# Paired eviction of narrow MLP column tiles, scaled V copies on GpSimd and a new planner table in an attention and token-MLP kernel

## The chip, the cores and the metric

The kernel runs on one core of one Trainium2 chip. Its time is device time in microseconds (us). The kernel before takes 757.67 us, the median of three runs (757.1 to 758.49).

## What is computed

The input x has 2048 tokens of 640 features, all in bf16. With xn = layernorm(x), the kernel computes x + s * g, where s is multi-head attention over xn (32 heads of 20 features) and g = silu of a token-mixing MLP of xn. The MLP multiplies along the tokens: 2048 to 1536, gelu, back to 2048. Cut to what matters:

```python
xn = _layernorm(x, axis=-1)
# attention A: H = 32, Dh = 20
q, k, v = split(xn @ wqkv)
p = softmax(einsum("bhqd,bhkd->bhqk", q, k) * Dh ** -0.5)
s = merge_heads(einsum("bhqk,bhkd->bhqd", p, v)) @ wo
# token MLP B, on xn normalised once more
h = _layernorm(xn, axis=-1)
u = gelu(einsum("bsd,sf->bdf", h, w1) + b1)
g = silu(transpose(einsum("bdf,fs->bds", u, w2) + b2))
return x + s * g
```

## The kernel before

**Attention.** Heads are taken in 8 groups of four, and a group in passes of 512 queries: 32 passes. A pass has 16 key chunks of 128 for each of four heads, 64 units; a unit is one score tile of 128 keys by 512 queries in one bank of PSUM. TensorE makes the scores (L1212, heads at four row positions of the array) and multiplies the exponentials with V into one accumulator bank (L1292, four heads at four column positions).

**Two ways to an exponential.** ACT takes two or three units per instruction (`emit_exp`, L1230, L1241). DVE takes quads: four heads of one key chunk, which must be one of the five in `RC`. It adds an offset to each score and writes it as a 16-bit integer whose bits, read as bf16, are roughly a power of two (`emit_op1`, L1252, four for a quad). Three more versions, shifted by 32, 64 and 96 steps of that integer, are made in one instruction of 2048 columns each (`emit_top`, L1276, three for a quad). The PV matmul then takes four versions in turn, with V and with three scaled copies of V, so that their sum averages out the error of the coarse exponential. The scaled copies are `vs_sb`, made in `vs_steps` (L751): three instructions for a head group, each over five key chunks of 88 columns, 440 together. Group 0 is done chunk by chunk at the start, 15 instructions of 88 columns; groups 1 to 7 are done three instructions each. `vs_sb` holds two groups, so those of group G wait until the PV matmuls of group G-2 are done.

**MLP.** `mlp_steps` (L791) computes 128 output rows j over 640 feature columns. The 640 are split into a part of 512 (part 0, one bank for each j) and a part of 128 (part 1). Two neighbouring j share a bank for part 1, side by side, and the instruction on L815 then evicts each of them: times one half, plus a bias that depends on j and the partition. The target is `zt_sb`, one half for even and one for odd j. `act_steps` (L822) applies gelu or silu to the pair. The weights come in pieces of 256 columns, 512 bytes a row (`dma_w1`, L771; `dma_w2`, L778), into two alternating buffers in `regA`.

**What sets the order of the work.** Nothing is decided on the chip. `schedule` runs a planner when the kernel is built: it keeps a clock for each engine, gives every step a cost in ns (`dv`, `dp`, `ac`, `mm` at L452 to L462, and the number at the end of each step), and always takes the earliest ready candidate of the earliest engine, by priority. A DMA's cost is its bytes at 355 bytes a ns (L476). The result is one fixed instruction list for each engine; `Prog._add` derives the semaphore waits. Jobs have a due time in passes (`at`), which spreads projections and MLP over the attention. All jobs compete with the scores for banks and engines: five banks are in two groups for ACT (three and two), one belongs to DVE, one is the accumulator, one serves jobs.

**The table.** `PLAN` (L317) has 129 rows of 14 digits. Every 16 units `tune` (L412) sets 14 options of the planner from the next row (`OPTS`, L301): how much slack a job may take ahead of ACT's deadline, whether DVE may take quads, from what DVE load on an ACT bank is lent to it, the sizes in which quads are accumulated, and more.

Of the kernel before, what the change touches and what calls it, by code (L numbers as in the profile page):

```python
# [7 lines left out]
ALU = mybir.AluOpType  # L8
AF = mybir.ActivationFunctionType

P = 128
# [249 lines left out]
class _Kern:  # L261
# [53 lines left out]
        ("GROT", (1, 0)),  # L315
    )
    PLAN = (  # L317
        "00000000000010", "00000000000000", "00000000000010", "00000000000000", "00000410000000", "10010410000100",
        "00004010011000", "20204010111000", "00000000000000", "02000020010010", "00000000000000", "00000010001000",
        "00000000000000", "01000120000000", "01003120000000", "00000000000000", "00000010000100", "00000310100000",  # L320
        "02020320011000", "02020320011000", "02120010011000", "00000220000100", "30000220000100", "02000010000000",
        "00000000000000", "00000000100000", "02000100100100", "01000120001010", "00000000000000", "00003300000000",
        "00000000000000", "01000000000010", "00004000000000", "10011000000000", "01022300000000", "00000000000000",
        "30020100000000", "02000010110000", "00000100000000", "00010100000110", "00001000000000", "20100000000100",
        "11000000000000", "00000000000000", "00001000010000", "10020000000000", "10020000010000", "10020010010000",
        "00000000000000", "22103000000000", "22103010000000", "01220100000100", "00000000000000", "00100000001000",
        "02000000100000", "01000300001000", "01000300001000", "00000000000000", "00100000001000", "00100400100000",
        "01000000001000", "00004000000000", "10002000010000", "01001400001010", "01021420000110", "00000300000000",
        "00000020000010", "00000000000000", "00000010001000", "10000100000000", "10000100000000", "10004100001000",
        "00004120000000", "00001010000000", "10011410000110", "11001200000110", "11001200100110", "00020000000000",  # L330
        "00000000000000", "00000000100100", "00200400100000", "02100010110010", "02101010100010", "01000000000000",
        "01000000000000", "00000000000000", "00000400000000", "00000000000000", "00000020001000", "00020320000000",
        "00000000000000", "01000010000000", "01000010000100", "20000000000100", "02000000000000", "12000000000000",
        "00001000101000", "00000000000000", "00200000010100", "00020020100000", "01003000000000", "22000000000000",
        "21210000000000", "00000000000000", "00200020110000", "00000000000000", "00200000000100", "00000000001000",
        "00020310000100", "00220020000010", "10224000000010", "31223410000010", "30200000000100", "00021000000010",
        "00100000001010", "01100000010010", "01204001000000", "01204100001000", "00204100000010", "02024120000000",
        "02024320000000", "02000200000000", "12000200010000", "00000000000000", "00001000100000", "00001000100000",
        "00000000001000", "10000000000000", "00000000000000",
    )  # L340
    PARTS = (2,)
    DX = (1, 2, 3)
# [74 lines left out]
    def schedule(self):  # L417
        pr, t, nc = self.prog, self.t, self.nc
        S, NB, NTB, F, FC, D, H, DH, NG, GH = (self.S, self.NB, self.NTB, self.F, self.FC, self.D,
                                               self.H, self.DH, self.NG, self.GH)  # L420
# [4 lines left out]
        wp_sb, zt_sb = t["wp_sb"], t["zt_sb"]  # L425
# [13 lines left out]
        def S_(name):  # L439
            s = sl.get(name)  # L440
            if s is None:
                s = sl[name] = _Slot(name)
            return s

        bank_slot = [S_(f"bank{i}") for i in range(8)]

        def ps(b, n=512, off=0):
            return ps_all[:, b * 512 + off:b * 512 + off + n]
# [3 lines left out]
        def mm(n):  # L452
            return max(n / 2.4 + 3.0, 60.0)

        def dv(n, rate=1.04):
            return 65.0 + n * rate

        def dp(n):
            return 66.0 + n * 1.04
# [291 lines left out]
        def vs_steps(G, rs):  # L751
            half = 0 if G < 2 else 1
            steps = []
            r0, n = rs[0], len(rs)
            for k in range(3):
                src = bass.AP(v_sb, (RC[r0] * H + G * 4) * 22, [[NB * H * 22, P], [(RC[1] - RC[0]) * H * 22, n], [1, 88]])
                dst = vs_sb[:, G % 2, k, r0:r0 + n, :]
                steps.append(("dve", lambda e, src=src, dst=dst, k=k: e.tensor_scalar(dst, src, self.AK[k + 1], None, ALU.mult),
                              [S_(f"v{half}_{RC[r]}") for r in rs], [S_(f"vs{G % 2}_{k}_{r}") for r in rs],
                              f"vs{G}", dv(88 * n, 0.51)))  # L760
            for r in rs:
                steps.append(("tag", f"vs{G}_{r}"))
            return steps

        def w1_ap(k):
            return bass.AP(regA, (k % 2) * NB * 256, [[NB * 640, P], [256, NB], [1, 256]])
# [4 lines left out]
        def dma_w1(k):  # L771
            src = B_w1[:, k * 256:(k + 1) * 256].rearrange("(b p) f -> p b f", p=P)
            dst = w1_ap(k)
            wr = [S_(f"wm{k % 2}")]
            return ("dma", lambda e: e.dma_start(dst, src), [], wr, f"dma_w1_{k}", S * 512,
                    [S_(f"x{b}") for b in range(NB)] if k < 2 else [])

        def dma_w2(k):  # L778
            src = B_w2[:, k * 256:(k + 1) * 256].rearrange("(fc p) s -> p fc s", p=P)
            dst = w2_ap(k)  # L780
            wr = [S_(f"wn{k % 2}")]
            return ("dma", lambda e: e.dma_start(dst, src), [], wr, f"dma_w2_{k}", F * 512,
                    [S_("wm0"), S_("wm1")] if k < 2 else [])

        def ztmp(i):
            return zt_sb[:, i % 2, 0, :]
# [4 lines left out]
        def mlp_steps(which, j, part):  # L791
            def make(bk):
                steps = []
                if which == 1:
                    wap, rows, nk = w1_ap(j // 2), regC, NB
                    rd = [S_(f"wm{(j // 2) % 2}")] + [S_(f"h{b}") for b in range(NB)]
                    bias, sb_ = b1h_sb, S_("b1h")
                else:
                    wap, rows, nk = w2_ap(j // 2), regB, FC
                    rd = [S_(f"wn{(j // 2) % 2}")] + [S_(f"gelu{f}") for f in range(FC)]  # L800
                    bias, sb_ = b2h_sb, S_("b2h")
                c0, n = (0, 512) if part == 0 else (512, 128)
                js = (j,) if part == 0 else (j - 1, j)
                for i, jj in enumerate(js):
                    col0 = (jj % 2) * 128
                    for k in range(nk):
                        steps.append(pcol(lambda a, b_, i=i: ps_all[a:b_, bk * 512 + i * n:bk * 512 + i * n + n],
                                          wap[:, k, col0:col0 + 128], rows[:, k, c0:c0 + n], k == 0, k == nk - 1, rd,
                                          [bank_slot[bk]], f"m{which}_{j}", mm(n)))
                for i, jj in enumerate(js):  # L810
                    if jj >= 2:
                        steps.append(("need", f"a{which}_{jj - 2}"))
                    z = ztmp(jj)
                    zw = [S_(f"z{jj % 2}_{part}")]
                    steps.append(("dve", lambda e, z=z, i=i, jj=jj: e.tensor_scalar(  # L815
                        z[:, c0:c0 + n], ps(bk, n, i * n), 0.5, bias[:, jj:jj + 1], ALU.mult, ALU.add),
                        [bank_slot[bk], sb_], zw, f"m{which}e_{j}", dp(n) + 60.0))
                    steps.append(("tag", f"m{which}_{jj}_{part}"))
                return steps
            return make  # L820
# [617 lines left out]
        for i, (b0, nb) in enumerate(LN):  # L1438
            rq = () if i < 4 else (f"xn{LN[i - 1][0] + LN[i - 1][1] - 1}",)
            steps = ln_steps(b0, nb)  # L1440
            k = next(n for n, x in enumerate(steps) if x == ("tag", f"lnp{b0}")) + 1
# [16 lines left out]
        for w in (1, 0):  # L1458
            src = A_wqkv[:, 640 * w + 256:640 * w + 640].rearrange("(kc p) f -> p kc f", p=P)
# [63 lines left out]
        for j in range(FC):  # L1523
# [6 lines left out]
            if j % 2 == 1 and j // 2 + 2 < FC // 2:  # L1530
                k = j // 2 + 2
# [4 lines left out]
        for j in range(NB):  # L1536
# [6 lines left out]
            if j % 2 == 1 and j // 2 + 2 < NB // 2:  # L1543
                k = j // 2 + 2
# [12 lines left out]
        for gb in range(4):  # L1557
            src = A_x[0, gb * 512:(gb + 1) * 512, :].rearrange("(b p) d -> p b d", p=P)
            dst = regA[:, gb * 4:(gb + 1) * 4, :]
# [377 lines left out]
        while True:  # L1937
# [40 lines left out]
            r, e = bt  # L1978
# [46 lines left out]
```

The softmax here doesn't subtract the row's maximum and nothing guards it: scores larger than these inputs give would overflow.

## Time and profile before

The profiled execution took 758.22 us; its span from the first to the last instruction is 756.4 us, at a granted TensorE clock of 1.0.

| engine | busy us | share | instructions |
|---|---|---|---|
| ScalarE (ACT) | 731.3 | 97% | 686 |
| TensorE (PE) | 726.6 | 96% | 10194 |
| VectorE (DVE) | 718.4 | 95% | 1319 |
| GpSimd (POOL) | 15.7 | 2% | 22 |

In a row of the profile's table of groups, a line number, an engine and an operation are followed by what is written and read, the shape, the count, then busy time in us, the mean of one in ns, and the engine's idle time just before these instructions with what ended most of it. In the views of waits, a row has the waiting engine and line, what it waited for, and the total in us, the number of times and the longest wait.

### The profile page before, as it was taken

The numbers are of one execution on the slowest core, as the hardware profiler recorded it, in microseconds if no ns is written. First come the engines' busy times: TensorE is split into PE (matmuls) and PEld (weight loads), VectorE is DVE, ScalarE is ACT, GpSimd is POOL, SyncE is SP. The second block draws the span as 40 slices with busy tenths as digits, with TensorE's granted clock in tenths as the row PEclk, the third lists the DMA queues.
The fourth block names the chain that finished last, engine by engine and source line by source line (L and its number), as shares of the span: only waits on it lengthen the run. The fifth ranks groups of instructions, "written<-read, shape, count | busy, mean of one in ns | idle before, by whom it ended". The sixth has DMA issues, their size and how long they took to land.

```text
span 756.4 us, 22917 instructions
## 1 busy us (share of the span) xinstructions
PE 726.6 (96%) x10194; PEld 245.9 (33%) x10194; DVE 718.4 (95%) x1319; ACT 731.3 (97%) x686; POOL 15.7 (2%) x22
## 2 busy tenths in 40 slices
PE   8899999999999999999999989999999899999997
PEld 6332233222332323323232233333333333322232
DVE  7799999999999999999999999999999898999996
ACT  4999999999999999999999999999999999999994
POOL 4200000000000000000000000000000000000001
PEclk9999999999999999999999999999999999999999
DMA  8694111101120302203010131331134510410002
GB/s 240 89 160 88 41 20 37 21 13 30 37 63 12 76 13 44 62 26 76 13 39 13 37 91 31 69 80 29 45 81 76 104 50 2 152 47 29 31 13 70
DMA packets 117143, 42.54 MB, mean 56 GB/s; under 512 B 75300, under 2 KB 115876, under 8 KB 116996
## 3 DMA queue, kind: packets, MB, share of 16 engines
q1 hardware_dynamic: 117044, 41.07, 24.2%
q8 instruction: 80, 1.31, 0.8%
q14 instruction: 19, 0.16, 0.1%
HBM read 26.37 MB, written 10.22 MB: 48 GB/s over the span
## 4 chain that ended last, share of the span: by engine, by line
ACT 67%; PE 23%; SPq 4%; DVE 3%; DMA 3%; POOL 1%; issue 0%; DVEq 0%; ACTq 0%
ACT pt_sb L1241 65%; PE ps_all L1212 7%; PE ps_all L1292 7%; PE ps_all L645 7%; SPq L906 3%; DMA xnT_sb<-regC 1%; PE ps_all L930 1%; DMA regA<-in_B_w_dram 1%; ACT zt_sb L836 1%; DMA wqk_sb<-in_A_wqkv_dram 1%; DVE dt_sb L1252 1%; PE ps_all L630 1%; POOL st_sb L567 0%; SPq L1425 0%; DVE regC L1615 0%
## 5 line engine op out<-in xcount | busy, mean ns | idle before, releaser
L1241 ACT ACTIVATE pt_sb<-ps_all 128x1024 bf16<-128x1024 f32 (+1 forms) x662 | 711.5, 1212 | 3.9 <-PE ps_all L1212 2.9
L1252 DVE TENSOR_SCALAR dt_sb<-ps_all 128x512 uint16<-128x512 f32 x496 | 330.8, 681 | 17.1 <-PE ps_all L1212 15.6
L1212 PE MATMUL ps_all<-qk_sb 32*128 32x512 bf16 x2048 | 286.6, 384 | 18.7 <-ACT pt_sb L1241 14.5
L1276 DVE TENSOR_SCALAR dt_sb<-dt_sb 128x2048 uint16<-128x2048 uint16 x372 | 245.9, 684 | 1.6
L1212 PEld LDWEIGHTS ps_all<-qk_sb 32*128 32x128 bf16 x2048 | 73.9, 91 | 276.4 <-ACT pt_sb L1241 193.0
L1292 PE MATMUL ps_all<-pt_sb,v_sb 128*21 128x512 bf16 x1552 | 123.6, 382 | 1.0 <-DVE v_sb L1045 1.0
L1292 PE MATMUL ps_all<-dt_sb,vs_sb 128*21 128x512 bf16 x1488 | 123.6, 381 | 0.3 <-DVE dt_sb L1276 0.2
L645 PE MATMUL ps_all<-regB,regA 128*32 128x128 bf16 (+1 forms) x1536 | 66.8, 301 | 1.5 <-DMA regA<-in_B_w_dram 1.2
L645 PE MATMUL ps_all<-regC,regA 128*32 128x512 bf16 (+1 forms) x1536 | 65.9, 301 | 0.0
L1292 PE MATMUL ps_all<-dt_sb,v_sb 128*21 128x512 bf16 x496 | 48.9, 385 | 0.6 <-DVE tr_sb L1408 0.3
L645 PE MATMUL ps_all<-xnT_sb,wqk_sb 128*32 128x512 bf16 x640 | 48.9, 382 | 0.3 <-DVE v_sb L1045 0.2
L1292 PEld LDWEIGHTS ps_all<-pt_sb,v_sb 128*21 128x21 bf16 x1552 | 29.1, 90 | 50.6 <-issue 38.5
L1292 PEld LDWEIGHTS ps_all<-dt_sb,vs_sb 128*21 128x21 bf16 x1488 | 31.6, 91 | 38.2 <-issue 18.8
L645 PEld LDWEIGHTS ps_all<-regB,regA 128*32 128x32 bf16 x1536 | 28.1, 96 | 28.5 <-issue 12.2
L645 PEld LDWEIGHTS ps_all<-regC,regA 128*32 128x32 bf16 x1536 | 28.5, 96 | 25.7 <-issue 11.7
L930 PE MATMUL ps_all<-wv_sb,xnT_sb 128*128 128x128 bf16 (+3 forms) x160 | 30.1, 302 | 0.1
L645 PE MATMUL ps_all<-wv_sb,xnT_sb 128*32 128x480 bf16 x320 | 23.6, 369 | 0.2 <-DVE v_sb L1045 0.2
L1408 DVE STREAM_TRANSPOSE tr_sb<-ps_all 128x512 f32<-128x512 f32 x31 | 21.9, 707 | 0.0
L645 PEld LDWEIGHTS ps_all<-xnT_sb,wqk_sb 128*32 128x32 bf16 x640 | 14.3, 95 | 20.0 <-issue 8.7
L1292 PEld LDWEIGHTS ps_all<-dt_sb,v_sb 128*21 128x21 bf16 x496 | 12.4, 90 | 23.7 <-issue 18.3
L815 DVE TENSOR_SCALAR zt_sb<-ps_all,b2h_sb 128x512 bf16<-128x512 f32 (+1 forms) x32 | 17.2, 543 | 1.4 <-PE ps_all L645 1.2
L1045 DVE CAST v_sb<-ps_all 128x480 bf16<-128x480 f32 (+1 forms) x24 | 14.3, 594 | 2.3 <-PE ps_all L738 2.1
(81 smaller groups left out, 291.0 us busy)
## 6 DMA issues: line engine op xcount, KB each, us to landing
regA<-in_B_w_dram SPq DMA_DIRECT2D x6, 1024.0 KB
regA<-in_B_w_dram SPq DMA_DIRECT2D x8, 768.0 KB
qk_sb<-qk_scratch_dram SPq DMA_DIRECT2D x56, 80.0 KB
qk_scratch_dram<-qs_sb SPq DMA_DIRECT2D x32, 128.0 KB
regA<-in_A_x_dram SPq DMA_DIRECT2D x6, 640.0 KB
ok_scratch_dram<-on_sb SPq DMA_DIRECT2D x96, 20.0 KB
out_dram<-regC SPq DMA_DIRECT2D x3, 640.0 KB
wqk_sb<-in_A_wqkv_dram SPq DMA_DIRECT2D x2, 480.0 KB
```

The lines of the kernel that those rows point to most:

```text
L630: steps.append(("pe", lambda e, dc=dc, lhsT=lhsT: e.matmul(ps(bk, n), lhsT, xnT_sb[:, dc, tb * 512 + c0:tb * 512 + c0 + n], start=(dc == 0 ...
L645: fns.append(lambda e, c=c, e_=e_: e.matmul(oc(c, e_), lhsT[:, c:e_], rhs, start=start, stop=stop, tile_position=(0, c)))
L815: steps.append(("dve", lambda e, z=z, i=i, jj=jj: e.tensor_scalar(z[:, c0:c0 + n], ps(bk, n, i * n), 0.5, bias[:, jj:jj + 1], ALU.mult, AL ...
L906: steps.append(("dma", lambda e, d=d, src=src: e.dma_start_transpose(d, src), [S_(f"okd{pass_of[(G, tb)]}_{g}") for G in range(L6) for g i ...
L930: steps.append(("pe", lambda e, c=c, k=k: e.matmul(ap, oT_sb[0:k, c, b * 128:(b + 1) * 128], wo_ap[0:k, c, c0:c0 + n], start=(opens and c ...
L1045: return lambda e: e.tensor_copy(dst, src)
L1212: pr.pe(lambda e, outp=outp, lhsT=lhsT, rhs=rhs, g=g: e.matmul(outp, lhsT, rhs, start=True, stop=True, tile_position=(32 * g, 0)), reads=[ ...
L1241: tk = pr.act(lambda e: e.activation(outp, inp, AF.Exp, scale=math.log(2.0) / 128.0), reads=[bank_slot[b] for b in banks[:n]], writes=[S_( ...
L1252: tk = pr.dve(lambda e: e.tensor_scalar(w, src, WOFF, 0.0, ALU.add, ALU.max), reads=[bank_slot[bk]], writes=[S_(f"dt{d['tl'][0]}_{g}")], n ...
L1276: tk = pr.dve(lambda e: e.tensor_scalar(dst, src, dk, None, ALU.add), reads=[S_(f"dt{b0}_{g}") for g in range(4)], writes=[S_(f"dt{b}_{g}" ...
L1292: pr.pe(lambda e: e.matmul(outp, lhsT, rhs, start=(k == 0), stop=last, tile_position=(0, 32 * g)), reads=reads, writes=[bank_slot[AB]], na ...
L1408: steps.append(("dve", lambda e: e.transpose(tr_sb[:, :], ps(AB)), [bank_slot[AB]], [S_("tr")], f"epT{q}", 632.0))
```

## The change

It has four parts.

1. `mlp_steps`: the two 128-column parts of a pair are evicted by one instruction of 2 x 128 columns. The bias is no longer a scalar for each partition but a second tensor operand, read with a step of zero along the columns.
2. `vs_steps`: the scaled V copies of groups 1 to 7 go to GpSimd, with a planned cost of 700 ns. Group 0 stays on DVE.
3. `dma_w1` and `dma_w2`: the planner counts 922 instead of 512 bytes for each row of weights. The transfers themselves are as before.
4. `PLAN`: a new table, of which four of the 129 rows equal the old ones at their place.

The first two are for taking work off DVE, the third for a truer picture of the weight loads in the planner, and the table fits the planner's choices to the new costs.

```diff
     PLAN = (
-        "00000000000010", "00000000000000", "00000000000010", "00000000000000", "00000410000000", "10010410000100",
...
+        "00010000000000", "02000000000000", "00000000000000", "00000020100100", "20104000000000", "10000000011000",
...
     )
@@ vs_steps
-                steps.append(("dve", lambda e, src=src, dst=dst, k=k: e.tensor_scalar(dst, src, self.AK[k + 1], None, ALU.mult),
+                steps.append(("pool" if G else "dve", lambda e, src=src, dst=dst, k=k: e.tensor_scalar(dst, src, self.AK[k + 1], None, ALU.mult),
                               [S_(f"v{half}_{RC[r]}") for r in rs], [S_(f"vs{G % 2}_{k}_{r}") for r in rs],
-                              f"vs{G}", dv(88 * n, 0.51)))
+                              f"vs{G}", 700.0 if G else dv(88 * n, 0.51)))
@@ dma_w1
-            return ("dma", lambda e: e.dma_start(dst, src), [], wr, f"dma_w1_{k}", S * 512,
+            return ("dma", lambda e: e.dma_start(dst, src), [], wr, f"dma_w1_{k}", S * 922,
@@ dma_w2
-            return ("dma", lambda e: e.dma_start(dst, src), [], wr, f"dma_w2_{k}", F * 512,
+            return ("dma", lambda e: e.dma_start(dst, src), [], wr, f"dma_w2_{k}", F * 922,
@@ mlp_steps
-                for i, jj in enumerate(js):
+                for jj in js:
                     if jj >= 2:
                         steps.append(("need", f"a{which}_{jj - 2}"))
+                if part:
+                    zp = zt_sb[:, :, 0, c0:c0 + n]
+                    bp = bass.AP(bias, j - 1, [[FC if which == 1 else NB, P], [1, 2], [0, n]])
+                    pp = ps(bk, 2 * n).rearrange("p (i n) -> p i n", i=2)
+                    steps.append(("dve", lambda e: e.scalar_tensor_tensor(zp, pp, 0.5, bp, ALU.mult, ALU.add),
+                                  [bank_slot[bk], sb_], [S_("z0_1"), S_("z1_1")], f"m{which}e_{j}", dp(2 * n) + 60.0))
+                    for jj in js:
+                        steps.append(("tag", f"m{which}_{jj}_{part}"))
+                    return steps
+                for i, jj in enumerate(js):
```

More of the change, by code (lines that the diff above doesn't have):

```diff
@@ L317 @@
     PLAN = (
-        "00000000000010", "00000000000000", "00000000000010", "00000000000000", "00000410000000", "10010410000100",
[L319 to L337, printed above, removed]
@@ L338 @@
-        "02024320000000", "02000200000000", "12000200010000", "00000000000000", "00001000100000", "00001000100000",
-        "00000000001000", "10000000000000", "00000000000000",
+        "00010000000000", "02000000000000", "00000000000000", "00000020100100", "20104000000000", "10000000011000",
+        "11003000110000", "00101000000000", "00000000000000", "02003100000000", "00000200000000", "00100200000000",
+        "00104200000000", "20104200100000", "00000000000000", "20102000100000", "20102000100100", "00000000000000",
@@ new lines @@
+        "00000000100000", "00021010100000", "30020020100000", "30020020110000", "10220020100000", "02100200000000",
+        "02000000000010", "11000000010000", "11000000110000", "11000100110100", "11002100110100", "00000020010000",
+        "00000000000000", "01020400101010", "00000220010000", "00000400000000", "00000300001000", "02120320001000",
+        "01103000001000", "01202020001000", "00000000000000", "00020000001000", "01014300010100", "01214420010100",
+        "00000000000000", "00200300001000", "00020010000000", "00000000000000", "02000000010000", "02000100001010",
@@ new lines @@
+        "00023010100010", "00223010100010", "00100010101000", "00203010001000", "00102000001000", "00000200110010",
+        "10000300110110", "00000000000000", "01100300000000", "00020000000010", "00000000000000", "10100000000000",
+        "20020000000000", "20020200001000", "00020400101000", "00100400000000", "00120420000100", "11100300100100",
+        "00020010001000", "00100000100000", "00000010000000", "21004200000000", "00000100000000", "00000000000000",
+        "02200000000000", "02200010010000", "10200010110010", "12200010110000", "00100000001000", "00000220000000",
@@ new lines @@
+        "10000220001000", "00200000000000", "00010020000000", "00000000000000", "00000110010100", "01010000000000",
+        "00200010010000", "00200410010000", "20022000101000", "00000010000100", "00220211000000", "00000000000000",
+        "00100200000000", "02200200000010", "00000020100100", "00000110000000", "00000320000000", "00000000000000",
+        "00021300000000", "00000020010100", "01221000000000", "00200000000000", "10001010000000", "00021010000000",
+        "00000000000000", "00210000101000", "00210000001000", "01000200000000", "01120000001100", "20000000000000",
@@ L340 @@
+        "01100020101000", "00000000000000", "00200400000000", "00200000000000", "32201000000000", "01020320100000",
+        "00000000000000", "00100000010000", "00000000000000", "00204300000000", "00224300100000", "00000000000000",
+        "30000010010000", "00014300001000", "30003300001000", "00000000000000", "00000000000000", "00001000000000",
+        "10100300001000", "10120301000000", "00000000000000",
     )
```

## The prediction

> **What bounds the kernel now.** I read the page's busy shares first, then the busy time by stage, then who ACT waits for, and last the costliest groups.
>
> ```profile
> PE 726.6 (96%) x10194; PEld 245.9 (33%) x10194; DVE 718.4 (95%) x1319; ACT 731.3 (97%) x686; POOL 15.7 (2%) x22
> ```
>
> Three engines are within two points of each other and GpSimd is free. Shares alone don't say which of the three sets the end, so I cut the middle into stages (columns: window, its length, busy us and instructions of PE, PEld, DVE, ACT, POOL, then clock, DMA share, GB/s).
>
> ```profile
> 39.00:100.00 61.00, 59.66 (x740) 18.61 (x738) 59.29 (x113) 60.99 (x58) 0.00 (x0) 1.00 0.48 85
> 100.00:200.00 100.00, 97.70 (x1285) 30.16 (x1282) 95.94 (x162) 99.74 (x95) 0.00 (x0) 1.00 0.11 23
> 300.00:400.00 100.00, 97.78 (x1481) 32.33 (x1479) 97.94 (x169) 99.96 (x95) 0.00 (x0) 1.00 0.20 44
> 500.00:600.00 100.00, 97.75 (x1651) 33.73 (x1648) 95.77 (x170) 99.83 (x96) 0.53 (x1) 1.00 0.37 76
> 600.00:700.00 100.00, 95.07 (x1235) 30.56 (x1237) 96.08 (x173) 98.60 (x93) 0.00 (x0) 1.00 0.17 56
> 700.00:742.00 42.00, 40.28 (x431) 12.53 (x423) 41.60 (x76) 41.61 (x39) 0.00 (x0) 1.00 0.10 33
> ```
>
> ACT is the full one. Adding the seven windows from 39 to 742 us (two are not shown: 200 to 300 with DVE 97.87, ACT 99.67; 400 to 500 with DVE 96.31, ACT 99.94), ACT idles 2.7 us of 703 and DVE 22.2 us. The waits of ACT and of DVE say what the idle time was:
>
> ```profile
> ACT pt_sb L1241 <- PE ps_all L1212: 2.9, 4, 1.3
> DVE dt_sb L1252 <- PE ps_all L1212: 15.6, 35, 1.3
> ```
>
> ACT's exponentials lose 2.9 us in all; DVE loses 15.6 us to scores that PE had not yet made. So the time is a start of 39 us, ACT's work, and a tail of 14 us; it shrinks if exponentials leave ACT. What an exponential costs on either side:
>
> ```profile
> L1241 ACT ACTIVATE pt_sb<-ps_all 128x1024 bf16<-128x1024 f32 (+1 forms) x662 | 711.5, 1212 | 3.9 <-PE ps_all L1212 2.9
> L1252 DVE TENSOR_SCALAR dt_sb<-ps_all 128x512 uint16<-128x512 f32 x496 | 330.8, 681 | 17.1 <-PE ps_all L1212 15.6
> L1276 DVE TENSOR_SCALAR dt_sb<-dt_sb 128x2048 uint16<-128x2048 uint16 x372 | 245.9, 684 | 1.6
> ```
>
> A unit is one 128x512 score tile of one head; there are 8 x 4 x 16 x 4 = 2048. DVE takes 496 (124 quads of four), ACT 1552, so 711.5/1552 = 0.458 us of ACT each. In the timeline DVE records follow one another 0.60 us apart although each lasts 0.68: a record overlaps the next by 0.08 us, so a DVE instruction occupies its record less 0.08. A quad is four of L1252 and three of L1276: 7 x 0.60 = 4.2 us of DVE. **One quad moved from ACT to DVE takes 4 x 0.458 = 1.83 us off ACT and so off the end**, as long as DVE and PE can carry it. (PE pays three more accumulations over four heads for it, 3 x 0.22 = 0.65 us.)
>
> **What the Trainium skill says.** "SBUF — State Buffer", Who interferes with whom: GpSimd's only SBUF ports are VectorE's second pair, an exclusive lock held for a whole instruction; VectorE instructions in a two-port mode contend, and those with two SBUF inputs contend with a GpSimd instruction that reads SBUF. The trace has one such meeting, in the tail: GpSimd's two additions run from 750.10 to 752.36.
>
> ```profile
> 750.10 2.26 POOL L1617 TENSOR_TENSOR regC<-regC,regA 128x512 bf16<-128x512 bf16 x2 [249.57 <-DVE regC L1615]
> 751.83 0.81 DVE L1633 TENSOR_TENSOR regC<-regC,regA 128x512 bf16<-128x512 bf16 x1
> 752.57 0.41 DVE L1617 TENSOR_TENSOR regC<-regC,regA 128x512 bf16<-128x512 bf16 x1
> ```
>
> The same addition of 512 columns (one strided) takes DVE 0.81 us beside GpSimd and 0.41 after it: it agrees. "VectorE: DVE Perf Modes", The perf-mode tier table, gives a 4x bf16 tensor_scalar of 2048 columns 693 ns; L1276 shows 684, so it is in that mode and takes the lock. "GPSIMD Engine Reference", 4.1 Engine selection, calls one-input GpSimd work roughly line-rate; no run here shows one that reads SBUF, only the memset of 1280 columns in 1.17 us and the two-input addition of 512 in 1.15 us.
>
> **The change part by part.** The rows that it touches:
>
> ```profile
> L758 DVE TENSOR_SCALAR vs_sb<-v_sb 128x440 bf16<-128x440 bf16 x21 | 7.1, 368 | 0.0
> L815 DVE TENSOR_SCALAR zt_sb<-ps_all,b2h_sb 128x128 bf16<-128x128 f32 x16 | 5.3, 342 | 0.1
> L815 DVE TENSOR_SCALAR zt_sb<-ps_all,b1h_sb 128x128 bf16<-128x128 f32 x12 | 3.8, 343 | 0.3 <-PE ps_all L645 0.3
> L945 DVE TENSOR_TENSOR regC<-ps_all,regC 128x128 bf16<-128x128 f32 x12 | 3.3, 272 | 0.0
> ```
>
> *Pairs.* 28 evictions of 128 columns (6 pairs in the first MLP half, 8 in the second) become 14 of 256. Two cost 2 x (0.342 - 0.08) = 0.52 us. For one of 256 I have two neighbours. On L815's line (128 columns 0.343, 512 columns 0.744) it lasts 0.343 + 0.401/3 = 0.477 and occupies 0.40. On the line of L945, which like the new instruction has a tensor and no pointer as second operand (0.272, and 0.679 for 512), it lasts 0.408 and occupies 0.33. The saving is 0.12 to 0.19; I take 0.16: 14 x 0.16 = 2.2 us of DVE. The joint wait for both halves adds nothing: both parts lie in one bank and are ready together, and the needs of both name the same earlier pair.
>
> *Scaled V copies.* 21 instructions leave DVE: 21 x (0.368 - 0.08) = 6.0 us. On GpSimd one of 440 columns takes, from the memset's slope (0.83 ns a column and some 0.1), 0.47 us at least; from the two-input addition 440/512 x 1.15 = 0.99 at most; I take the 0.7 that the new planner writes. Each copy waits for the previous readers, the PV matmuls of group G-2; behind it on GpSimd's queue lie only other copies, one memset for the output weights (0.63 us at 499.9, first used by the output projection much later) and the tail's additions. Its readers are PV matmuls about a pass later (a pass is some 22 us, three copies 2.1 us), so this latency is hidden. What is not hidden is the lock. L1276 is 34% of DVE's time, instructions with two SBUF inputs and other two-port ones some 6% more. A copy that meets them either waits itself, free of cost, or makes DVE's next locking instruction wait out its rest. Ends: 0 and 0.5 us for each; I take 0.25: 21 x 0.25 = 5.3 us back. Net gain of this part 0.7 us, between -4.5 and 6.
>
> *Planner's costs.* A weight load for the MLP is planned at 922 instead of 512 bytes a row. The trace says why: at 594.47 a load of 768 KB takes 6.57 us to the matmul that waits for it, PE stands 1.2 us, and then ACT shows 1.29 us idle at 603.37, half of its idle time in the whole middle. A planner that knows this can put other work there. I count the 1.3 us as gone.
>
> *Table.* It has 129 rows of 14 choices, of which only four rows are as before. It can't be costed from rows. What counts is how many quads it lets DVE take. DVE gains 2.2 + 0.7 = 2.9 us and has 22.2 us idle; a quad needs 4.2, so one more fits without better packing, and I take 125. The columns that steer this directly are nearly as before (rows that switch DVE's share off go from 1 to 2, the no-loan rows from 6 to 7), which speaks against a big move.
>
> Sum: 757.67 - 1.83 (one quad) - 1.3 (weight stall) = 754.5 us. The DVE savings don't enter by themselves: DVE isn't what ACT waits for.
>
> **The rivals.**
> *The table packs better (three or more quads).* Three quads take 5.5 us off: 757.67 - 5.5 = 752.2. For: 22 us of idle DVE. Against: PE idles only 2 to 5% per stage, loses time at each switch of its tiling, and DVE's idle time is waiting for PE.
> *Nothing.* 124 quads as before and the freed DVE time turns into more waits on L1212; ACT's work stays 711.5: 757.5. For: DVE already waits 35 times.
> *Slower.* The lock costs more than the copies did, the order is fixed at build time and knows nothing of it, so a DVE instruction that is 0.3 to 0.7 us late holds a lent bank, then a score matmul, then ACT; or the new table, searched on a model, gives DVE a quad less. A quad less is +1.83, and 21 copies of which one in five holds ACT for 0.5 us are 2.1 us: 761.6 for both, 760 for most mixtures. For: ACT has no buffer beyond its two groups of banks.
>
> **How the numbers follow.** Forecast 0.42; better packing 0.16; nothing 0.20; slower 0.22. The time is the forecast's, 754.5. Down, the range takes in better packing to four quads with no stall mended (757.67 - 7.3 = 750.4, so 750.5); up, the usual mixture of the slower case, 760. Some 0.15 to 0.2 is left out, nearly all of it above 760 or under 750.5. The bound of 0.2% is 1.5 us: faster 0.42 + 0.16 = 0.58, same 0.20, slower 0.22.
>
> **What would show it.** L1252 with 500 instructions instead of 496, L1241's busy time near 709.7 and its idle time under 3 us. L815's 128-column rows gone, and a row of 14 with 256 columns at 0.41 to 0.48 us. GpSimd with 21 more instructions of 0.5 to 1.0 us. L1276's mean over 684 ns, by 5.3/372 = 14 ns if the lock costs what I take. It is wrong if L1252 shows 496 or fewer, or if ACT's waits for L1212 grow past 5 us.

## The result and the profile after

The changed kernel takes 761.9 us (median of four runs, 761.6 to 762.89) against 757.82 before: a ratio of 1.0056, 95% interval 1.0039 to 1.0074, so 4.1 us slower. The prediction said 754.5 and 750.5 to 760.0. Ratios here and below leave out one execution far above the rest, of 2327.2 us among e4's 21.

The page of the kernel after, busy us and instructions of each engine:

```profile
PE 731.5 (96%) x10178; PEld 248.3 (33%) x10178; DVE 714.2 (94%) x1284; ACT 731.8 (96%) x685; POOL 47.9 (6%) x43
```

DVE has 4.2 us less to do, ACT as much as before (731.3), and the span is 3.6 us longer. The groups of the page, in the columns used before, say what became of the DVE time:

```profile
L1251 ACT ACTIVATE pt_sb<-ps_all 128x1024 bf16<-128x1024 f32 (+2 forms) x661 | 711.8, 1219 | 7.2 <-PE ps_all L1222 6.8
L1262 DVE TENSOR_SCALAR dt_sb<-ps_all 128x512 uint16<-128x512 f32 x496 | 332.8, 684 | 27.5 <-PE ps_all L1222 26.1
L1286 DVE TENSOR_SCALAR dt_sb<-dt_sb 128x2048 uint16<-128x2048 uint16 x372 | 250.0, 695 | 1.9
L758 POOL TENSOR_SCALAR vs_sb<-v_sb 128x440 bf16<-128x440 bf16 x21 | 31.8, 1515 | 371.2 <-PE ps_all L1302 205.8
```

(L1251, L1262, L1286, L1222 and L1302 are the lines that were L1241, L1252, L1276, L1212 and L1292 before.) Four things are to be seen. L1262 still has 496 instructions: the new table gives DVE not one quad more. DVE's waits for scores grew by 10.5 us, from 15.6 to 26.1: 4.0 of them lie in the stall shown below, and the other 6.5 are more than the 4.2 us that it was spared. A copy on GpSimd lasts 1.5 us on average, not 0.7. And ACT's wait for scores grew from 2.9 to 6.8 us, 3.9 us, close to the whole loss.

Where ACT waits is shown by the stages (window, length, busy us and instructions of PE, PEld, DVE, ACT, POOL, clock, DMA share, GB/s), first by hundreds and then around 200 us:

```profile
100.00:200.00 100.00, 98.73 (x1291) 30.11 (x1287) 95.65 (x161) 99.67 (x95) 0.00 (x0) 1.00 0.11 23
200.00:300.00 100.00, 95.20 (x1416) 31.71 (x1416) 93.36 (x158) 95.64 (x90) 13.91 (x9) 0.98 0.18 42
300.00:400.00 100.00, 98.05 (x1453) 32.23 (x1453) 96.00 (x162) 99.62 (x93) 4.31 (x3) 1.00 0.20 43
500.00:600.00 100.00, 97.72 (x1565) 33.36 (x1564) 93.68 (x158) 99.48 (x94) 10.39 (x7) 1.00 0.34 73
600.00:700.00 100.00, 98.05 (x1370) 33.06 (x1362) 96.39 (x172) 99.86 (x94) 0.00 (x0) 1.00 0.18 55
...
200.00:210.00 10.00, 7.26 (x95) 2.25 (x99) 8.73 (x16) 8.30 (x8) 5.33 (x4) 1.00 0.32 67
210.00:220.00 10.00, 10.00 (x209) 4.62 (x209) 7.25 (x13) 7.81 (x8) 4.01 (x3) 0.83 0.28 78
```

The kernel before, from 200 to 300 us:

```profile
200.00:300.00 100.00, 98.51 (x1593) 33.59 (x1590) 97.87 (x173) 99.67 (x93) 0.00 (x0) 1.00 0.20 44
```

One stage carries nearly all of the loss: from 200 to 300 us ACT is busy 4.0 us less than before. In 200 to 220 us PE, DVE and ACT all have holes while GpSimd is at work, and the granted clock has a mean of 0.83 in the second half. Read in steps of 1 us it is 0.50 from 211 to 214; in all it is at half speed for 10 x 0.17/0.5 = 3.4 us. From 300 to 400 and from 500 to 600 us, where copies run too, ACT idles 0.34 and 0.35 us more than before. From 600 to 700 us it idles 0.14 us instead of 1.4: the stall on the weights is gone.

The timeline there, in order of time (start, length, engine, line, what, count, idle time before and its releaser):

```profile
203.83 0.60 DVE L1055 CAST v_sb<-ps_all 128x480 bf16<-128x480 f32 x1
204.51 8.26 POOL L758 TENSOR_SCALAR vs_sb<-v_sb 128x440 bf16<-128x440 bf16 x5 [152.98 <-DVE v_sb L1055]
206.65 0.39 PE L1302 MATMUL ps_all<-dt_sb,vs_sb 128*21 128x512 bf16 x4
208.24 0.40 PE L1302 MATMUL ps_all<-dt_sb,vs_sb 128*21 128x512 bf16 x4 [1.20 <-POOL vs_sb L758]
209.95 0.40 PE L1302 MATMUL ps_all<-dt_sb,vs_sb 128*21 128x512 bf16 x4 [1.31 <-POOL vs_sb L758]
210.61 0.40 PE L1222 MATMUL ps_all<-qk_sb 32*128 32x512 bf16 x4
211.05 1.45 ACT L1251 ACTIVATE pt_sb<-ps_all 128x1536 bf16<-128x1536 f32 x1 [2.74 <-PE ps_all L1222]
```

This is the chain. V of key chunk 14, the last that group 2's copies need, is evicted from PSUM at 203.83. Only then do the three copies start. (The row of five holds these three and the first two of group 3.) They take 1.91, 1.69 and 1.63 us while DVE is at work; the fourth, which starts at 209.87 when DVE has nothing to do, takes 1.31. Group 2's first quad is already at hand: its first two versions go through PV from 206.43 and 206.65, and the third and the fourth wait 1.20 and 1.31 us for copies two and three. Behind them in TensorE's queue stand the scores, so ACT waits 2.74 us, and then 0.81 and 0.34 us more in and just after the stretch at half clock. Together that is 3.9 us.

### The profile page after: what moved, and what is told of

Read it like the earlier page. It is cut to its first block, busy times and chain, and to the rows that moved or that the text cites. A ratio compares the mean times of both kernels' runs of the same rounds, so it can differ in the third digit from the quotient of the medians.

```text
span 760.0 us, 22883 instructions
## 1 busy us (share of the span) xinstructions
PE 731.5 (96%) x10178; PEld 248.3 (33%) x10178; DVE 714.2 (94%) x1284; ACT 731.8 (96%) x685; POOL 47.9 (6%) x43
## 4 chain that ended last, share of the span: by engine, by line
ACT 58%; PE 26%; DVE 12%; DMA 2%; POOL 1%; issue 0%; SPq 0%; DVEq 0%
ACT pt_sb L1251 57%; PE ps_all L1222 8%; PE ps_all L645 8%; PE ps_all L1302 8%; DVE dt_sb L1262 4%; DVE dt_sb L1286 3%; DMA xnT_sb<-regC 1%; PE ps_all L940 1%; POOL vs_sb L758 1%; PE ps_all L630 1%; ACT zt_sb L851 1%; DMA regA<-in_A_x_dram 0%; ACT zt_sb L846 0%; DVE tr_sb L1418 0%; DVE regC L550 0%
## 5 line engine op out<-in xcount | busy, mean ns | idle before, releaser
L1251 ACT ACTIVATE pt_sb<-ps_all 128x1024 bf16<-128x1024 f32 (+2 forms) x661 | 711.8, 1219 | 7.2 <-PE ps_all L1222 6.8
L1262 DVE TENSOR_SCALAR dt_sb<-ps_all 128x512 uint16<-128x512 f32 x496 | 332.8, 684 | 27.5 <-PE ps_all L1222 26.1
L1222 PE MATMUL ps_all<-qk_sb 32*128 32x512 bf16 x2048 | 291.6, 385 | 16.2 <-ACT pt_sb L1251 11.6
L1286 DVE TENSOR_SCALAR dt_sb<-dt_sb 128x2048 uint16<-128x2048 uint16 x372 | 250.0, 695 | 1.9
L1222 PEld LDWEIGHTS ps_all<-qk_sb 32*128 32x128 bf16 x2048 | 76.1, 91 | 274.6 <-ACT pt_sb L1251 183.1
L1302 PE MATMUL ps_all<-dt_sb,vs_sb 128*21 128x512 bf16 x1488 | 123.8, 382 | 3.4 <-POOL vs_sb L758 2.5
L1302 PE MATMUL ps_all<-pt_sb,v_sb 128*21 128x512 bf16 x1552 | 122.4, 382 | 0.8 <-DVE v_sb L1055 0.8
L645 PE MATMUL ps_all<-regC,regA 128*32 128x512 bf16 (+1 forms) x1536 | 70.6, 305 | 0.2 <-DVE qs_sb L1055 0.2
L645 PE MATMUL ps_all<-regB,regA 128*32 128x128 bf16 (+1 forms) x1536 | 69.1, 301 | 0.2 <-DVE zt_sb L817 0.2
L758 POOL TENSOR_SCALAR vs_sb<-v_sb 128x440 bf16<-128x440 bf16 x21 | 31.8, 1515 | 371.2 <-PE ps_all L1302 205.8
L1302 PE MATMUL ps_all<-dt_sb,v_sb 128*21 128x512 bf16 x496 | 49.1, 386 | 0.8 <-DVE tr_sb L1418 0.8
L645 PE MATMUL ps_all<-xnT_sb,wqk_sb 128*32 128x512 bf16 x640 | 46.9, 381 | 0.3 <-DVE qs_sb L1055 0.2
L1302 PEld LDWEIGHTS ps_all<-dt_sb,vs_sb 128*21 128x21 bf16 x1488 | 31.0, 91 | 44.3 <-issue 22.0
L1302 PEld LDWEIGHTS ps_all<-pt_sb,v_sb 128*21 128x21 bf16 x1552 | 28.3, 90 | 48.0 <-issue 34.6
L1302 PEld LDWEIGHTS ps_all<-dt_sb,v_sb 128*21 128x21 bf16 x496 | 12.4, 90 | 23.8 <-issue 17.4
```

Source lines behind the costliest of these rows:

```text
L645: fns.append(lambda e, c=c, e_=e_: e.matmul(oc(c, e_), lhsT[:, c:e_], rhs, start=start, stop=stop, tile_position=(0, c)))
L758: steps.append(("pool" if G else "dve", lambda e, src=src, dst=dst, k=k: e.tensor_scalar(dst, src, self.AK[k + 1], None, ALU.mult), [S_(f" ...
L1222: pr.pe(lambda e, outp=outp, lhsT=lhsT, rhs=rhs, g=g: e.matmul(outp, lhsT, rhs, start=True, stop=True, tile_position=(32 * g, 0)), reads=[ ...
L1251: tk = pr.act(lambda e: e.activation(outp, inp, AF.Exp, scale=math.log(2.0) / 128.0), reads=[bank_slot[b] for b in banks[:n]], writes=[S_( ...
L1262: tk = pr.dve(lambda e: e.tensor_scalar(w, src, WOFF, 0.0, ALU.add, ALU.max), reads=[bank_slot[bk]], writes=[S_(f"dt{d['tl'][0]}_{g}")], n ...
L1286: tk = pr.dve(lambda e: e.tensor_scalar(dst, src, dk, None, ALU.add), reads=[S_(f"dt{b0}_{g}") for g in range(4)], writes=[S_(f"dt{b}_{g}" ...
```

## The experiments

Theory 1 is this one stall. Its rivals: the port that GpSimd shares with DVE slows DVE everywhere (theory 2), or the new table makes a longer schedule by itself (theory 3). The planner's choices depend on its costs, so undoing a part in the source would change everything. Experiments e2 to e5, e7 and e10 therefore leave the planner's decisions alone and change only what is issued: the instruction orders of TensorE, ACT and the DMA queue are those of the kernel they start from. Ratios are to the kernel before on the same chip.

| run | what is different | time us | ratio, 95% interval |
|---|---|---|---|
| e11 | changed kernel again | 761.80 | 1.0058 (1.0042 to 1.0074) |
| e2 | group 2's copies short | 757.49 | 1.0009 (1.0002 to 1.0017) |
| e3 | copies of groups 3 to 7 short | 759.95 | 1.0044 (1.0031 to 1.0056) |
| e4 | group 2's copies split | 757.82 | 1.0012 (1.0005 to 1.0020) |
| e5 | all copies on DVE | 759.57 | 1.0040 (1.0028 to 1.0053) |
| e7 | pairs undone | 762.43 | 1.0063 (1.0047 to 1.0080) |
| e8 | pairs alone, old table | 766.02 | 1.0114 (1.0096 to 1.0131) |
| e9 | e4, true cost, other table | 754.40 | 0.9970 (0.9958 to 0.9981) |
| e10 | e9's order, both parts undone | 756.99 | 0.9999 (0.9988 to 1.0011) |

### e2: group 2's copies cut short

```diff
-            r0, n = rs[0], len(rs)
+            r0, n = rs[0], 1 if G == 2 else len(rs)
```

> The changed kernel (761.9 us) with the three GpSimd copies of head group 2 cut from 440 to 88 columns; every other instruction and its order is as in the changed kernel. It leaves out the scaled V copies of four of five key chunks of group 2 (stale values are used). Theory 1, one stall: TensorE waits for these three copies at 208 us, the scores queued behind it come late, ACT idles 3.9 us there, and that is the whole loss. Then this kernel takes 758 us (757.3 to 758.8), and ACT's waits for scores fall from 6.8 to about 3 us. Theory 2, the shared port: 21 copies slow DVE all over the kernel; three shorter ones give back at most 0.6 us, so 761.3. Theory 3, the new table makes a longer schedule whatever the copies cost: 761.5 to 762.

Measured 757.49, ratio 1.0009. Three instructions of 21 carry 0.0056 - 0.0009 = 0.47%, 3.5 us of the 4.1. In the waits of ACT (total us, times, longest):

```profile
ACT pt_sb L1251 <- PE ps_all L1222: 3.0, 9, 0.8
```

It is back from 6.8 to 3.0. Theory 1 holds for most of the loss; a port that slows DVE everywhere, or a longer schedule whatever the copies cost, can't give this.

### e3: the other groups' copies cut short

The same edit with `G > 2`.

> The changed kernel with the copies of groups 3 to 7 (15 of the 21) cut from 440 to 88 columns, those of groups 1 and 2 left whole; all orders as in the changed kernel. It leaves out the scaled V copies of four of five key chunks of groups 3 to 7. Theory 1 (one stall on group 2): nothing changes, 761.3 to 762. Theory 2 (shared port): most of the port's cost goes, L1286's mean falls from 695 towards 687 ns, and the time by up to 2.9 us, to 759. Theory 3 (table): 761.5 to 762.

Measured 759.95, ratio 1.0044: 0.12%, 0.9 us, better than the changed kernel, with the stall still there. The intervals overlap, so a gain in time is not shown, but the mean of DVE's port-taking instruction moved as the shared port would have it:

```profile
L1286 DVE TENSOR_SCALAR dt_sb<-dt_sb 128x2048 uint16<-128x2048 uint16 x372 | 246.5, 684 | 1.9
```

684 ns, as in the kernel before, against 695 with whole copies in the first profile and 691 in e11, the same kernel again. Theory 2 is a real effect on DVE, of 7 to 11 ns an instruction; what it costs in time these runs don't fix. 0.47 from e2 and 0.12 from this add up to 0.59%, the whole loss within its interval.

### e4: the copies split, with a complete result

```diff
-            add_job(f"vs{G}", vs_steps(G, list(range(NR))), vtag + ((f"pvG{G - 2}",) if G >= 2 else ()), 28.0,
-                    at=(4 * G - 1.0 if G < NG - 1 else 24.0))
+            for n, rs in enumerate(((0, 1, 2, 3), (4,)) if G == 2 else (tuple(range(NR)),)):
+                rq = tuple(f"v{0 if G < 2 else 1}_{RC[r]}" for r in rs) + ((f"pvG{G - 2}",) if G >= 2 else ())
+                add_job(f"vs{G}_{n}", vs_steps(G, list(rs)), rq, 28.0, at=(4 * G - 1.0 - (1.5 if n == 0 and G == 2 else 0.0) if G < NG - 1 else 24.0))
```

> The changed kernel with group 2's copies split: the four key chunks whose V is ready early are copied by three instructions of 352 columns as soon as the fourth is there, and only the last chunk (three instructions of 88 columns) waits for its late V. Complete result. All other engines have the same instructions in the same order. Theory 1: the late part shrinks from three times 1.5 us to three times about 0.4, the stall goes, 758 (757.3 to 758.8). Theory 2: three copies more on the shared port, 762. Theory 3: 761.5 to 762.

Measured 757.82, ratio 1.0012. The timeline: four chunks are copied 26 us before the late one, and the twelve matmuls on the scaled copies no longer wait.

```profile
177.79 4.10 POOL L758 TENSOR_SCALAR vs_sb<-v_sb 128x352 bf16<-128x352 bf16 x3 [126.66 <-DVE v_sb L1055]
206.25 0.82 PE L1302 MATMUL ps_all<-dt_sb,vs_sb 128*21 128x512 bf16 x12
```

So the stall needed both: copies more than twice as long as planned, and all of them held back for the last fifth of V. (An estimate: at the planned 0.7 us each from 204.51 on, the three would have ended at 206.6, when the first of those matmuls began.) Without it the changed kernel is still no faster than before. Its DVE spends 23.1 us waiting for scores:

```profile
L1262 DVE TENSOR_SCALAR dt_sb<-ps_all 128x512 uint16<-128x512 f32 x496 | 331.2, 680 | 24.7 <-PE ps_all L1222 23.1
```

### e5: all copies back on DVE

```diff
-                steps.append(("pool" if G else "dve", lambda e, src=src, dst=dst, k=k: e.tensor_scalar(dst, src, self.AK[k + 1], None, ALU.mult),
+                steps.append(("dve", lambda e, src=src, dst=dst, k=k: e.tensor_scalar(dst, src, self.AK[k + 1], None, ALU.mult),
...
-                              f"vs{G}", 700.0 if G else dv(88 * n, 0.51)))
+                              f"vs{G}", 0.0 if G else dv(88 * n, 0.51)))
```

> The changed kernel with all scaled copies back on DVE, placed in its fixed order where the planner sees them at no cost; TensorE, ACT and the DMA queue have the same instructions in the same order. Theory 1: the three copies of group 2 take 0.9 us in place of 4.5 and the stall all but goes; DVE has 6 us more of its own work but no port to share: 758 to 759. Theory 2: the port is the loss, all of it goes: 758, with L1286 at 684 ns again. Theory 3: 761 to 762.5.

Measured 759.57, ratio 1.0040, a miss: above the 758 to 759 of theories 1 and 2 and below theory 3's 761. The port's cost is gone (L1286 at 683 ns) and no matmul waits for a copy, yet it is 0.28%, 2.1 us, slower than e4, which has the copies on GpSimd and no stall. ACT's waits for scores are 4.5 us, where e4 has 3.6. The largest stands at the old place:

```profile
207.65 0.65 DVE L1055 CAST v_sb<-ps_all 128x480 bf16<-128x480 f32 x1
209.24 1.45 ACT L1251 ACTIVATE pt_sb<-ps_all 128x1536 bf16<-128x1536 f32 x1 [0.69 <-PE ps_all L1222]
```

The three copies stand on DVE ahead of the eviction of chunk 15, TensorE waits 0.64 us for that eviction, and the scores behind it come 0.69 us late for ACT. So in this order the GpSimd placement does save time, and more than its port costs, once the stall is gone.

### e6: the copy by itself

```diff
+        for k in range(3):
+            pr.pool(lambda e, k=k: e.tensor_scalar(vs_sb[:, 1, k, :, :], bass.AP(wp_sb, 0, [[1280, P], [256, 5], [1, 88]]),
+                                                   self.AK[k + 1], None, ALU.mult), reads=[S_("wp0"), S_("wp1")],
+                    writes=[S_(f"vs1_{k}_{r}") for r in range(NR)], name="lone", cost=0.0)
```

> The changed kernel with three extra copies of 128x440 on GpSimd near the start, from a zeroed tile and into a place that is overwritten later, while DVE runs no instruction that needs the shared port. It measures the copy by itself. If GpSimd's own speed sets the 1.5 us, these three also follow one another about 1.4 to 1.5 us apart. If waiting for the port makes up half of it, they are 0.7 to 0.9 us apart. The first layernorms come some 4 us later, so the time is not of interest.

The timeline near the start:

```profile
2.87 4.05 POOL L514 TENSOR_SCALAR vs_sb<-wp_sb 128x440 bf16<-128x440 bf16 x3
6.87 2.83 POOL L518 MEMSET v_sb<- 128x1024 bf16 x1
7.04 2.68 DVE L547 TENSOR_SCALAR st_sb<-st_sb 128x2 f32<-128x2 f32 x1
```

Three copies take 4.05 us, 1.35 each with the gaps and 1.31 by itself, with DVE's layernorm statistics beside them. (The one run took 766.14 us; the copies stand ahead of the first layernorms, so its time says nothing here.) In the kernel after, the shortest, median and longest of the 21 are, in ns:

```profile
L758 POOL TENSOR_SCALAR vs_sb<-v_sb x21: 1306/1500/1911, 47.1 to 564.8; 128x440 bf16<-128x440 bf16 x21
```

So most of the 1.5 us is GpSimd's own time, and 0.2 us on average is added beside DVE. In the stall it was more: 1.91 + 1.69 + 1.63 is 1.3 us over three times 1.31, so about a quarter of the time that these copies took there is what the port, most likely, added. The third row of the first view shows the port from DVE's side: an instruction on two columns, elsewhere 0.15 to 0.18 us, takes 2.68 us and ends with GpSimd's memset. Its wait stands inside its record and not in the idle time before it.

### e7: the pairs undone in place

```diff
-                    steps.append(("dve", lambda e: e.scalar_tensor_tensor(zp, pp, 0.5, bp, ALU.mult, ALU.add),
+                    two = lambda e: [e.tensor_scalar(ztmp(jj)[:, c0:c0 + n], ps(bk, n, i * n), 0.5, bias[:, jj:jj + 1], ALU.mult, ALU.add) for i, jj in enumerate(js)][-1]; steps.append(("dve", two,
```

> The changed kernel with each of the 14 paired evictions of 256 columns written as the two evictions of 128 that it replaced, at the same place; all orders as in the changed kernel. Pairs occupy DVE 0.415 - 0.08 = 0.335 us against 2 x 0.26 = 0.52, so DVE does 14 x 0.185 = 2.6 us more here. If DVE time in the fixed order costs end time at the rate at which the 21 copies did when they went back to DVE (6.1 us more of DVE, 2 us more of time than with the stall gone), this kernel is 0.8 us slower than the changed one, ratio 1.0066 to before. If DVE's idle time hides it, the ratio stays at 1.0056.

Measured 762.43, ratio 1.0063, where the changed kernel has 1.0056. The 0.5 us between them lies within either interval: in this order the pairs bring at most a few tenths of a percent. The pair itself costs what its neighbours on other lines said (kernel after, groups with shapes kept apart):

```profile
L817 DVE SCALAR_TENSOR_TENSOR zt_sb<-ps_all,b2h_sb 128x256 bf16<-128x256 f32 x8 | 3.3, 415 | 0.0
```

### e8: the pairs alone with the old table

This is the kernel before with the `mlp_steps` part of the diff and nothing else.

> The kernel before with the paired evictions alone: old table, copies on DVE, old weight costs. It does strictly less DVE work than before. But the planner decides anew from changed costs with a table that was fitted to others, and now gives DVE 488 units in place of 496, two quads fewer. If the count of quads sets the time, ACT has 8 units more at 0.458 us: 757 + 3.7 = 760.7 at least, more where ACT has to wait. If the saved DVE time counts, it is 756 or less.

Measured 766.02, ratio 1.0114: less DVE work for each step, and 8.6 us slower.

```profile
PE 729.5 (95%) x10156; PEld 247.7 (32%) x10174; DVE 710.0 (93%) x1291; ACT 737.6 (96%) x692; POOL 15.6 (2%) x22
...
L1262 DVE TENSOR_SCALAR dt_sb<-ps_all 128x512 uint16<-128x512 f32 x488 | 325.8, 682 | 30.2 <-PE ps_all L1222 28.5
```

DVE's share fell to 488 units. ACT is busy 6.3 us longer than before, 3.7 of which are eight more units at 0.458 us; the rest is a little more for each unit (717.7/1560 = 0.460 us). ACT's waits for TensorE are 5.9 us against 3.2, another 2.7. A saving that the table was not fitted to is worse than none here.

### e9: two more quads

Starting from e4, the planned cost of a copy is set to what it measured, and the table is searched again: a beam search over its rows on the planner's own clocks.

```diff
-                              f"vs{G}", 700.0 if G else dv(88 * n, 0.51)))
+                              f"vs{G}", 200.0 + 260.0 * n if G else dv(88 * n, 0.51)))
     PLAN = (
-        "00010000000000", "02000000000000", "00000000000000", "00000020100100", "20104000000000", "10000000011000",
+        "00000400000000", "00000400000000", "00000400000000", "00000400000000", "00004000100000", "00004300100110",
...
```

> The changed kernel with group 2's copies split as in e4, the planner's cost of a copy set to what it measured (200 ns and 260 ns for each 88 columns, 1.5 us for 440), and a table searched again by me with these costs. The planner now gives DVE 504 units, two quads more than before and after. If the number of quads sets the time, as the prediction had it, ACT has 8 units less: its exponentials fall from 711.5 to about 707.8 us and the time to 757 - 3.7 = 753.3, and to 751 if the planner's own gain against the changed kernel (6.7 us) comes through. If another engine has become the bound, ACT's waits for scores grow by as much and the time stays at 756 to 758.

Measured 754.40, ratio 0.9970 (0.9958 to 0.9981): faster than both kernels, by 2.3 us than the kernel before.

```profile
PE 722.9 (96%) x10148; PEld 245.0 (33%) x10162; DVE 720.8 (96%) x1298; ACT 728.0 (97%) x694; POOL 47.2 (6%) x46
...
L1262 DVE TENSOR_SCALAR dt_sb<-ps_all 128x512 uint16<-128x512 f32 x504 | 335.1, 680 | 12.0 <-PE ps_all L1222 10.2
```

504 units on DVE, ACT's busy time down 3.3 us from before, DVE's waits for scores at 10.2 us. Two quads were to bring 3.7 us, and the kernel gained 2.3; the interval reaches from 1.4 to 3.2, which is less than ACT's rate says, and what took the rest isn't settled. The planner's 6.7 us against the changed kernel came through as 1.0056 - 0.9970 = 0.86%, 6.5 us, but partly by luck: 3.5 of those are the stall, of which the planner's figure for the changed kernel knew nothing.

### e10: are the two parts what makes the room?

> The kernel of e9 in its fixed order, with both DVE savings undone in place: all scaled copies on DVE, the pairs as two evictions each. TensorE, ACT and the DMA queue have e9's orders. DVE has 6.1 + 2.6 = 8.7 us more to do. In the changed kernel's order 6.1 us of copies cost about 2 us and 2.6 us of evictions some 0.5. If the two parts are what makes room for the two more quads, this kernel takes 757 (e9 was 754.4, ratio 0.997). If the table alone did it, DVE's idle time hides the 8.7 us and it stays at 754 to 755.

Its edits are those of e5 and e7, on e9. Measured 756.99, ratio 0.9999: the whole gain of e9 is lost. TensorE and ACT have e9's orders here, with 504 units on DVE, so the 8.7 us of DVE work that the pairs and the GpSimd copies remove are worth 0.29%, 2.2 us, in this order. ACT's busy time is 1.2 us above e9's and its waits for scores are 3.5 us, not 2.3. That a search made for a kernel without the two parts would not find such a table is not shown.

### e11: the changed kernel again

> The changed kernel once more, beside e10 on one chip, so that the experiments' ratios have one to stand against: 1.0056 as before, with the stall at 208 us (ACT's waits for scores 6 to 8 us).

761.80, ratio 1.0058, as in the first comparison.

## Why the prediction was wrong

Both signs of being wrong that the prediction named came: L1252's successor shows 496, and ACT's waits passed 5 us. Its sum missed by 7.4 us. The quad's 1.83 us did not come, the 1.3 us of the weight stall did not come through in the total, and the 3.9 us of group 2's stall stood nowhere in the sum; together these are 7.0.

**What bounds the kernel: right, with its proviso.** ACT's work and ACT's waits account for the times. The changed kernel has 1552 units on ACT as before and 3.9 us more of waiting for scores; e9 has eight units less and is 2.3 us faster; e8 has eight more and is 8.6 us slower. But e10 has eight less too and is no faster than before: the 1.83 us a quad hold only "as long as DVE and PE can carry it", and are ACT's share alone, not what a new order adds or takes.

**One quad more: wrong.** "One more fits without better packing, and I take 125." It is 124. That a quad would fit is true (e9 has 126), but the table of the change doesn't use the room, and DVE's 6.5 us of added waiting outside the stall say where its savings went. Room on an engine isn't a quad until the order uses it. The rival "nothing" described this step, and e4, which has it without the stall, lands at 1.0012.

**"This latency is hidden": wrong, and the main error.** Two terms failed at once. The copy was bounded by 0.47 and 0.99 us from a memset and a two-input addition; it takes 1.31 alone and 1.6 to 1.9 in the stall. And "waits itself, free of cost" did not hold there either: the 1.3 us by which these three copies were longer beside DVE lie on the chain that ACT waited for. And "its readers are PV matmuls about a pass later" looked at the job's due time, not at what the copy waits for. For group 2 that is V of chunk 14, evicted at 203.83 us, 2.8 us before the first scaled matmul. The trace before shows the same lateness in its timeline of DVE:

```profile
201.38 0.65 DVE L1045 CAST v_sb<-ps_all 128x480 bf16<-128x480 f32 x1
203.14 0.95 DVE L758 TENSOR_SCALAR vs_sb<-v_sb 128x440 bf16<-128x440 bf16 x3
```

Chunk 14 came late there too, at 201.38 (the last eviction is that of chunk 15, at 204.61), but three copies took 0.95 us. With the right size of the copy this term would have been at least 3 x 1.31 us after the last V, against the 2.1 us that the planner believed. The trace before has a sign of that size too, though it is another instruction: GpSimd's one-input AFFINE_SELECT of 128x128 bf16, at 1.41 us, takes 0.29 us, 2.3 ns a column. The prediction says that no run shows one-input work that reads SBUF.

**The shared port and the speed of GpSimd.** The Trainium skill's rule on the shared port, "SBUF — State Buffer", Who interferes with whom, was confirmed (e3, e6). My size for it was not far off, in part by luck, since it was taken for copies of half the length: 5.3 us of DVE time expected, 372 x 7 to 11 ns = 2.6 to 4.1 us measured on L1286. In time e3 puts it at 0.9 us, within the noise. What its "GPSIMD Engine Reference", 4.1 Engine selection, says of one-input work, roughly line-rate, doesn't hold for this instruction: 1.31 us for 440 columns is 3.0 ns a column, where the memset's slope is 0.83. The measurement decides.

**Right as forecast:** the pair at 0.415 us, in the range of 0.41 to 0.48, and so 14 x (0.52 - 0.335) = 2.6 us of DVE where 2.2 were taken; L1286's mean up by 7 to 11 ns where 14 were named.

**The weight stall: right in its place, wrong in the sum.** It is gone, with ACT idle 0.14 us from 600 to 700 us. But with group 2's stall away as well, the kernel should have been 1.3 us faster than before, and e2 and e4 are 0.7 and 0.9 us slower. Some of that is the 0.34 and 0.35 us that ACT lost from 300 to 400 and 500 to 600 us; the rest is not traced. No run separates the 922 bytes from the new table, so which of them removed the stall stays open.

**Two readings of the prediction.** The windows that the prediction adds up are eight, not seven; its 2.7 and 22.2 us are right. The weight load issued at 594.47 has its matmul at 601.09, which is 6.62 us and not 6.57.

**The rival that came closest** was "slower", for a different reason than the one given: not the port's hold on DVE, and not a quad less, but one wait for a copy with the scores queued behind it. Its 0.22 was too small because the wait was taken for hidden.

**What stays open.** e4's 0.12% above before is no more than the 0.9 us that e3 puts on the port, but that figure is within the noise and was measured beside the stall. What the pairs alone are worth in e9's order was not separated from the copies; e10 undoes both. How much of the stall's 3.9 us is the half clock that followed it was not tried. Of ACT's three waits the last two, 1.15 us, stand in and just after that stretch. Whether true costs alone, or the new search alone, would have given e9's table was not tried either.

## What to carry to other kernels

When work moves to an idle engine, ask for each instruction when its last input is there and when its first reader comes, and what is queued in order behind that reader. An idle engine hides latency only if the input isn't late; splitting the work so that the early inputs go first took the whole stall away here. In this kernel, whose order is fixed by a planner, time saved on an engine that is not the bound turned into waiting; it paid only in an order that was searched again with measured costs (e9, e10), and with an unfitted order it cost more than it brought (e8).

## What the runs showed of the hardware that was not expected

- A tensor_scalar of 128x440 bf16 on GpSimd takes 1.31 us by itself (e6) and up to 1.91 beside DVE; DVE does it in 0.37. The copies of 352 and of 88 columns in e4 take 1.31 and 0.66 us.
- A DVE instruction on two columns took 2.68 us beside a GpSimd memset of 2.83 us (e6). Its wait is in its record, so it shows as a longer mean and not as idle time.
- After TensorE's holes at 206 to 210 us in the kernel after, the granted clock fell to half for 3.4 us. It fell there in each of the five profiles that have the stall (for 6.8 us in e3, 3.4 in the kernel after, e6, e7 and e11) and in none of e2, e4 and e5. Holes of this size are not the only thing that goes before it: e4's clock is 0.50 from 448 to 451 us after a gap of 0.96 us at 447, while the kernel after has a gap of 1.0 us between 440 and 460 us and a clock of 1.0. What sets it off stays open. In e4, which has no holes from 206 to 210 us, the mean clock of 200 to 220 us is 1.0:

```profile
200.00:210.00 10.00, 9.77 (x205) 4.04 (x197) 10.00 (x18) 9.99 (x10) 5.58 (x5) 1.00 0.31 66
210.00:220.00 10.00, 9.58 (x139) 3.15 (x136) 9.78 (x17) 9.89 (x11) 1.31 (x1) 1.00 0.39 107
```
